# Scoring part of batch 0 through 128x32 TensorE tiles, with a check of the row sums and a second program behind it

## The chip, the cores and the metric

The kernel runs on one core of a Trainium2 chip. A core has five engines that run side by side and meet through semaphores: TensorE (PE, matrix multiplications into PSUM, with PEld as its weight loads), VectorE (DVE), ScalarE (ACT), GpSimd (POOL) and SyncE (SP). POOL and SP start DMA transfers here, ACT two of them. PSUM has eight banks of 128 x 512 float32. The metric is the device time of one execution in microseconds (us); lower is better. Weights of a matmul are rows x columns: a "128x32 tile" multiplies with 128 rows of weights and 32 output rows, and occupies a quarter of the array.

## The reference

```python
scale = 1.0 / np.sqrt(q.shape[-1])
scores = scale * np.matmul(q, k.transpose(0, 1, 3, 2))
scores = np.einsum('bhij,hg->bgij', scores, w_pre)
scores = scores - np.max(scores, axis=-1, keepdims=True)
attn = np.exp(scores)
attn = attn / (np.sum(attn, axis=-1, keepdims=True) + 1e-09)
attn = np.einsum('bhij,hg->bgij', attn, w_post)
out = np.matmul(attn, v)                      # b, head, row, 64
x = out.transpose(0, 2, 1, 3).reshape(8 * 448, 768)
h = np.maximum(x @ w_in, 0.0)
return (h * h) @ w_out
```

8 batches, 12 heads, 448 rows, head size 64; w_in is 768 x 2048, w_out 2048 x 768. Twelve heads of scores are mixed by `w_pre` ahead of the softmax and by `w_post` behind it. The subtraction of the row's maximum cancels in exact arithmetic; it keeps the exponential in range.

## The kernel before

**The scheme.** The program is planned by itself. Python code emits tasks with costs and dependencies; `_Plan` places them. TensorE's order is written out by hand: `ORDER` is a string in which each digit names one of ten streams (0 transposes, 1 QK, 2 pre, 3 post, 4 AV, 5 direct, 6 and 7 FFN-in, 8 and 9 FFN-out), and the next unit of that stream goes next. The planner gives copies out of PSUM to ACT or DVE, whichever ends earlier by its costs, and picks the PSUM banks. Every engine then runs its list in order.

**Attention.** The 448 rows of a batch are cut into 45 chunks of ten rows, so that a chunk has 10 x 12 heads = 120 rows of scores. For most chunks three steps make the scores. `emit_QK` multiplies a tile of rows by all keys, one pair of heads at a time, and copies the result into `stage`, rows on partitions (lines 460 and 461 are the copy helper, on ACT and on DVE). `emit_rel` moves a chunk by DMA from SP (line 954) to `dring`, with heads and rows of the chunk on 120 partitions. `emit_pre` (line 977) mixes the heads there with `wk1`, in 64x64 tiles. Behind it, `after_pre` takes the exponential with the row sum (ACT, line 994), the reciprocal (line 1008), and folds it into the `w_post` weights (line 1015, POOL). `emit_post` (line 1047) transposes and mixes again, with two copies into `a2t`. `emit_AV` (lines 1104 and 1125) multiplies by v. The exponential is taken without the maximum.

**The first 22 chunks of batch 0** go another way, since there is no earlier batch whose FFN could run beside them. `emit_scale` (line 834, DVE) multiplies q with `w_pre` into `w_out_sb` and `h2t`, which are not in use yet; `emit_direct` (line 856) adds up six full matmuls of 128x128 over 448 keys, which yields mixed scores in the layout of a chunk at once, without QK, relay and pre. The exponential reads that bank.

**FFN.** `emit_F1` multiplies by w_in (for batches 0 and 1 in whole 128x128 matmuls, line 1173; behind them in pairs of 64-row halves, line 1194), then relu (lines 1225 and 1226) and the square (line 1235) into `h2t`. `emit_F2` multiplies by w_out in halves (line 1316), `emit_last` the last two tiles whole (line 1265). The forms of tiles in use are called full (128x128), row (two of 64x128), quad (four of 64x64) and cols (two of 128x64).

Of the kernel before, what the change touches and what calls it, by code (L numbers as in the profile page):

```python
# [8 lines left out]
DT = mybir.dt  # L9
# [14 lines left out]
EVENTS = {"tr": 0.12, "qk": 0.72, "di": 0.2, "po": 0.61, "pr": 1.1, "av": 0.43, "o0": 0.43}  # L24
# [3 lines left out]
INF = float("inf")  # L28
ORDER = (
    "0001155500055555555555555555513155511155555331555533355551135555552005113555555330023324"  # L30
    "2443310041316261116722326772267633227713367333761142441114223667227631167713226671136713"
    "3277620029333912293921812283383338240024442002661118111833381118132672226773136713376224"
    "2444227761136711166333620027622813822383383337771422444200116667733002277622181183118133"
    "8339122922933912291191139333924244422163613731711631622007227363216372227610016733720208"
    "1383338113822291911393119224244422383138311831384222444223621617311716331620027337226336"
    "2127372001636217337220093191119131922833831181138242444222919313933392242444228318331811"
    "1833622267317216362200733733622167200173622367131720029319131931192228181338113822283833"
    "1842244442444238161336220073373362226761171716337610026733724244412812283382020839111911"
    "3913392291192229319138333811382424442283611673317622673137163167122762226733791229339213"
    "98338242444228338338222868633837226773667733677646444876766776678766776879989999899888"  # L40
# [12 lines left out]
class _Task:  # L53
# [3 lines left out]
                 "done", "bias", "sync", "group", "instrs", "issued", "later", "two")  # L57

    def __init__(self, name, engine, fn, deps, after, cost, prio, sem, seminc, mode, dma,
# [18 lines left out]
        self.sync = ()  # L78
        self.done = self.issued = False
# [9 lines left out]
class _Group:  # L89
# [4 lines left out]
    def __init__(self, n):  # L94
        self.n = n
        self.banks = None
        self.readers = [[] for _ in range(n)]


class _Plan:  # L100
# [44 lines left out]
    def _commit(self, t, e, start):  # L145
# [5 lines left out]
        self.free[e] = start + held  # L151
        t.end = start + lat
# [93 lines left out]
    def _commit_pe(self, t, start):  # L246
        if t.mode != self.mode:
            self.mode = t.mode
        g = t.group
        if g is not None and g.banks is None:  # L250
            _, got = self.find(g.n, self.free[PE])
            g.banks = sorted(got)
            for i, readers in zip(g.banks, g.readers):
                for d in self.bank_users[i]:
                    if d not in t.deps:
                        t.deps.append(d)
                self.bank_users[i] = readers
                self.age += 1
                self.bank_age[i] = self.age
# [8 lines left out]
    def next_unit(self, order, at):  # L268
        if at >= len(order):
            return None  # L270
        t = self.streams[int(order[at])][0]
        if t.nwait:
            return None
        est = max(self.free[PE], t.avail)
        if t.group is not None and t.group.banks is None:
            est = max(est, self.find(t.group.n, self.free[PE])[0])
        if t.mode != self.mode:
            est = max(est, self.free[PE] + MODE_SWITCH)
        return (est, t) if est < INF else None

    def run(self, order=""):
        self.start()
        at = 0
        while True:
# [15 lines left out]
            if f is not None and (best is None or f[0] <= best[0]):  # L300
# [3 lines left out]
                self.streams[int(order[at])].pop(0)  # L304
                at += 1
                self._commit_pe(f[1], f[0])
# [12 lines left out]
def bass_talking_heads_attention__then__ffn_squared_relu_kernel(  # L319
# [18 lines left out]
    ND = 22  # L338
    NDW = 16
    DH = 4  # L340
# [23 lines left out]
    with ExitStack() as es:  # L364
# [12 lines left out]
        NFULL = 2  # L377
# [8 lines left out]
        wq = sb("wq", [128, NP, H, H5], DT.bfloat16)  # L386
        wall = sb("wall", [128, NP, 2, H], DT.float32)
# [5 lines left out]
        rowsum = sb("rowsum", [128, NPS, 1], DT.float32)  # L393
# [17 lines left out]
        zrow = sb("zrow", [128, S], DT.bfloat16)  # L411
# [4 lines left out]

        def Sm(name):
            return _Sem(nc.alloc_semaphore(name), name)
# [5 lines left out]
        sem_z = Sm("dz")  # L424
        sem_qk = [[Sm("dqk%d_%d" % (i, x)) for x in range(2)] for i in range(3)]
        sem_v = Sm("dv")
        sem_wq = Sm("dwq")
# [3 lines left out]
        sem_last = Sm("olast")  # L431
        sem_out = [Sm("oslot%d" % i) for i in range(NOS)]

        plan = _Plan(NB)

        def c_pe(t):
            return {PE: (t, t + 190.0)}

        def c_ev(cols):
            return {ACT: (cols / 1.2 + 65.0, cols / 1.2 + 175.0),  # L440
                    DVE: (cols / 0.96 + 72.0, cols / 0.96 + 160.0)}

        def add(name, engine, fn, deps, cost, prio, mode=None, group=None, instrs=0):
            return plan.add(name, engine, fn, deps, cost, prio, "ctr", 1, mode, group=group,
                            instrs=instrs)

        events = {}

        def unit(s, name, fn, deps, ns, mode, group, mms):
            kind = name[:2]  # L450
            was = events.get(kind, 0.0)
            events[kind] = was + EVENTS.get(kind, 0.5)
            n = 2 * mms + int(events[kind]) - int(was)
            t = add(name, PE, fn, deps, c_pe(ns), 0, mode, group, n)
            s.append(t)
            return t

        def copy(eng, en, o, i_):
            if en == ACT:
# [1051 lines left out]
```

## Time and profile before

| | us |
|---|---|
| median of 3 runs | 526.3 (523.89 to 526.61) |
| the profiled execution | 521.03 |
| its span, first to last instruction | 519.0 |
| ACT exponentials, 360 | 191.1 busy, 555 ns each |
| PE FFN-out in halves, 1664 | 152.0 busy |
| PE FFN-in in halves, 1344 | 121.9 busy |
| DVE copies into a2t, 192 | 117.3 busy |

The page gives for each engine the busy time and its share of the span; then the span in 40 slices, a digit for tenths:

```profile
PE   7998999999999999999999999999999999999997
DVE  6966989889889677978897778975897668865430
ACT  3688999889988889898998889988878886887310
PEclk9999999999999999999999999999999999999999
```

The clock of TensorE was granted in full throughout. The chain of work is followed back from the last instruction: at each step to what released it, or to the instruction before it on its engine. Busy time of PE holds the latency of its last matmul, so neighbouring rows overlap.

### The profile page before, as it was taken

What the parts mean: (1) busy time and instruction counts of PE and PEld (TensorE: products, weight loads), DVE (VectorE), ACT (ScalarE), POOL (GpSimd) and SP (SyncE); (2) the same over time, 40 slices, a digit from 0 to 9 for tenths busy, and PEclk for the clock granted to TensorE, in tenths of its full rate; (3) what the DMA queues carried; (4) which work ended last, traced back from release to release, by engine and by line L of the source; (5) the groups of instructions that cost most, each with busy time, mean ns of one, the idle gap of its engine ahead of it and who ended that gap; (6) DMA issues with size and microseconds to landing.
All of it is one profiled execution on the core that took longest, in us unless ns stands there. A gap on an engine that the chain in (4) does not pass through costs nothing.

```text
span 519.0 us, 23210 instructions
## 1 busy us (share of the span) xinstructions
PE 505.7 (97%) x9632; PEld 320.0 (62%) x9632; DVE 397.4 (77%) x999; ACT 418.5 (81%) x1206; POOL 204.1 (39%) x404
## 2 busy tenths in 40 slices
PE   7998999999999999999999999999999999999997
PEld 3455767577776564666555665566556565568874
DVE  6966989889889677978897778975897668865430
ACT  3688999889988889898998889988878886887310
POOL 9913445425651455134632357124722332332000
PEclk9999999999999999999999999999999999999999
DMA  8999999746984689647984679537965557632003
GB/s 156 198 217 170 187 192 194 168 109 146 167 177 106 144 162 183 134 87 164 175 163 91 141 165 182 128 72 156 192 103 111 125 131 139 123 87 66 4 23 99
DMA packets 82560, 71.85 MB, mean 138 GB/s; under 512 B 13434, under 2 KB 79946, under 8 KB 82458
## 3 DMA queue, kind: packets, MB, share of 16 engines
q0 software_dynamic: 36944, 32.81, 38.8%
q1 hardware_dynamic: 45226, 37.38, 30.1%
q8 instruction: 77, 1.26, 1.0%
q10 hardware_dynamic: 288, 0.20, 0.1%
q14 instruction: 25, 0.20, 0.1%
HBM read 45.70 MB, written 11.01 MB: 109 GB/s over the span
## 4 chain that ended last, share of the span: by engine, by line
PE 87%; DMA 5%; DVE 4%; ACT 2%; issue 1%; SPq 1%; POOL 0%; POOLq 0%; DVEq 0%
PE ps L1316 26%; PE ps L1194 18%; PE ps L1047 7%; PE ps L977 7%; PE ps L1173 6%; PE ps L1125 6%; PE ps L908 6%; PE ps L856 5%; DMA dring<-stage 3%; PE ps L1265 2%; DVE stage L461 2%; PE ps L759 1%; DMA qraw<-in_q_dram 1%; PE ps L1104 1%; ACT pring L994 1%
## 5 line engine op out<-in xcount | busy, mean ns | idle before, releaser
L994 ACT ACTIVATE pring<-ps 128x448 bf16<-128x448 f32 x360 | 191.1, 555 | 16.3 <-PE ps L977 10.3
L1316 PE MATMUL ps<-w_out_sb,h2t 64*128 64x384 bf16 x1664 | 152.0, 323 | 0.6 <-issue 0.6
L1015 POOL TENSOR_TENSOR wk2s<-wk2b,rinv 128x120 bf16<-128x120 bf16 (+1 forms) x179 | 69.8, 392 | 189.8 <-DVE rinv L1008 188.6
L461 DVE CAST a2t<-ps 128x480 bf16<-128x480 f32 (+1 forms) x192 | 117.3, 640 | 14.7 <-PE ps L1047 13.2
L1194 PE MATMUL ps<-xt,w_in_sb 64*128 64x448 bf16 (+2 forms) x1344 | 121.9, 323 | 0.2
L461 DVE CAST stage<-ps 128x448 bf16<-128x448 f32 (+1 forms) x174 | 104.5, 617 | 15.4 <-PE ps L908 11.5
L460 ACT ACTIVATE stage<-ps 128x448 bf16<-128x448 f32 (+1 forms) x186 | 96.6, 551 | 23.0 <-PE ps L908 21.1
L1316 PEld LDWEIGHTS ps<-w_out_sb,h2t 64*128 64x128 bf16 x1664 | 77.1, 94 | 52.4 <-issue 3.6
L460 ACT ACTIVATE a2t<-ps 128x480 bf16<-128x480 f32 (+1 forms) x176 | 92.8, 574 | 13.6 <-PE ps L1047 13.2
L1194 PEld LDWEIGHTS ps<-xt,w_in_sb 64*128 64x128 bf16 x1344 | 62.2, 94 | 40.4 <-PE ps L977 2.2
L1348 POOL DMA_DIRECT2D out_dram<-osb x59 | 37.1, 634 | 111.3 <-ACT pring L994 42.2
L994 ACT ACTIVATION_READ_ACCUMULATOR pring<-ps 128x1 f32 x360 | 79.0, 219 | 0.0
L1047 PEld LDWEIGHTS ps<-wk2s,pring 60*128 60x128 bf16 x2880 | 56.1, 93 | 21.4 <-issue 3.1
L1047 PE MATMUL ps<-wk2s,pring 60*128 60x60 bf16 x2880 | 61.1, 187 | 1.0 <-issue 0.3
L1226 DVE TENSOR_SCALAR h1t<-ps 128x448 bf16<-128x448 f32 (+2 forms) x102 | 49.0, 488 | 16.5 <-PE ps L1194 14.1
L1008 DVE RECIPROCAL rinv<-rowsum 128x2 f32<-128x2 f32 (+1 forms) x184 | 29.1, 158 | 35.9 <-ACT pring L994 35.0
L977 PE MATMUL ps<-dring,wk 60*64 60x448 bf16 (+1 forms) x676 | 54.5, 362 | 1.5 <-DVE stage L461 0.6
L1235 DVE TENSOR_TENSOR h2t<-h1t 128x448 bf16<-128x448 bf16 (+2 forms) x176 | 52.6, 332 | 0.5 <-ACT h1t L1225 0.2
L908 PE MATMUL ps<-qkt 64*128 64x448 bf16 (+1 forms) x360 | 49.8, 354 | 1.4 <-issue 1.4
L1225 ACT ACTIVATE h1t<-ps 128x448 bf16<-128x448 f32 (+2 forms) x74 | 32.9, 456 | 19.7 <-PE ps L1194 18.0
L1173 PE MATMUL ps<-xt,w_in_sb 128*128 128x220 bf16 (+1 forms) x384 | 41.7, 260 | 0.1
L1173 PEld LDWEIGHTS ps<-xt,w_in_sb 128*128 128x128 bf16 x384 | 34.6, 98 | 5.7 <-DVE h1t L1226 0.9
(59 smaller groups left out, 419.3 us busy)
## 6 DMA issues: line engine op xcount, KB each, us to landing
dring<-stage SPq DMA_DIRECT2D x309, 105.0 KB
out_dram<-osb POOLq DMA_DIRECT2D x45, 192.0 KB, 4.0
qraw<-in_q_dram POOLq DMA_DIRECT2D x42, 112.0 KB, 5.5
kraw<-in_k_dram POOLq DMA_DIRECT2D x42, 112.0 KB, 5.3
w_in_sb<-in_moe_w_in_dram POOLq DMA_DIRECT2D x8, 384.0 KB, 12.7
w_out_sb<-in_moe_w_out_dram POOLq DMA_DIRECT2D x8, 384.0 KB, 8.7
vraw<-in_v_dram POOLq DMA_DIRECT2D x21, 128.0 KB, 5.1
vraw<-in_v_dram POOLq DMA_DIRECT2D x21, 96.0 KB, 5.3
```

Source lines behind the costliest of these rows:

```text
L460: return eng.activation(o, i_, AF.Copy)
L461: return eng.tensor_copy(o, i_)
L908: r_ = eng.matmul(ps[y * w:(y + 1) * w, g.banks[x], 0:S], qkt[r0:r0 + 64, pb, p + y, 0, i0:i0 + w], qkt[r0:r0 + 64, pb, p + y, 1, :], star ...
L977: r_ = eng.matmul(ps[64 * y:64 * y + 64, gr.banks[x], 0:S], wk1[64 * x:64 * x + 64 - R0 * x, :], dring[64 * x:64 * x + 64 - R0 * x, (g0 + ...
L994: return eng.activation(pring[:, pr, 0:S], ps[:, gr.banks[x], 0:S], AF.Exp, accum_out=rowsum[:, pr, :])
L1015: return eng.tensor_tensor(wk2s[:, p0:p0 + n, :], i0.to_broadcast([128, n, PR]), rinv[:, p0:p0 + n, :].to_broadcast([128, n, PR]), ALU.mult)
L1047: r_ = eng.matmul(ps[:, gr.banks[x], o0:o0 + PR], pring[64 * x:64 * x + PR, pr + y, j0:j0 + 2 * PJ], wk2s[64 * x:64 * x + PR, pr + y, :], ...
L1173: r_ = eng.matmul(ps[:, g.banks[0], 0:n], w_in_sb[:, ft, t * 128:(t + 1) * 128], xt[:, ft, c0:c1], start=(ft == 0), stop=(ft == NFT - 1))
L1194: r_ = eng.matmul(ps[:, g.banks[x], 0:n], w_in_sb[64 * y:64 * y + 64, ft, t * 128:(t + 1) * 128], xt[64 * y:64 * y + 64, ft, c0:c1], start ...
L1226: return eng.tensor_scalar(h1t[:, s, 0:n], ps[:, g.banks[x], 0:n], 0.0, None, op0=ALU.max)
L1235: return eng.tensor_tensor(h2t[:, t16, o0:o0 + n], h1t[:, s, 0:n], h1t[:, s, 0:n], ALU.mult)
L1316: r_ = eng.matmul(ps[:, g.banks[hh], 0:FH], h2t[64 * y:64 * y + 64, t16, col:col + 128], w_out_sb[64 * y:64 * y + 64, t16, hh * FH:(hh + 1 ...
```

## The change

Five things change together.

1. Thirty chunks of batch 0 (`ND` 22 to 30) go a new way. `emit_spread` copies q into `qz`, a zeroed part of `h2t`, so that for each chunk and pair of heads ten columns stand in one of eight places of 32 columns, zero elsewhere. `emit_spr` multiplies in eight matmuls of 128x32 weights, two for each of four column groups, accumulated; one copy brings the bank to `dring`; `emit_pre` mixes it with `wkf` in one full matmul. The products with `w_pre` and `emit_direct` are gone, and so are the zeroing of `dring` by DMA and the load of `w_pre` to all partitions; four small loads bring `wrepf`.
2. The remaining 15 chunks of batch 0 are scored as before, from two tiles of rows.
3. Every QK unit of 128 rows, every FFN-in pair and every FFN-out tile but the last two can be run in two forms; the letters a to j in `ORDER` choose the other one (quad for QK, full for the FFN). The order is new throughout.
4. Row sums of all chunks are kept. At the end DVE tests that each lies between 1e-30 and 1e30, a DMA from SP turns the 128 results into one row, and a last reduction makes a flag.
5. The whole program is built twice; the second one takes the row's maximum first. Each engine runs up to a point near its end, waits for the flag, loads it, and either jumps behind the second program and ends its list, or ends its list and runs the second program. PE does that behind its last unit; ACT from tasks planned 4 us behind the flag, DVE 8 us, POOL 0.5, SP 0.

```diff
-    ND = 22
+    ND = 30
+EVENTS = {..., "sp": 0.3, ...}
+TURN = {ACT: 4000.0, DVE: 8000.0, POOL: 500.0, SP: 0.0}
...
+            def emit_spread(p):
+                for x, (k, o) in enumerate(places(p)):
+                    def fn(eng, en, x=x, k=k, o=o):
+                        rows = slice(64 * x, 64 * x + 64)
+                        i_ = qkt[rows, 0, p, 0, 0:ND * CH].rearrange("p (c a) -> p c a", a=CH)
+                        return copy(eng, en, qz[rows, :, k, o:o + CH], i_)
...
+            def emit_spr(c, parts):
...
+                    for n, col, p in todo:
+                        r_ = eng.matmul(ps[32 * col:32 * col + 32, g.banks[0], 0:S],
+                                        qz[:, c, 2 * col + n, :], qkt[:, 0, p, 1, :],
+                                        start=(n == 0), stop=(n == 1))
...
+                def fn_sev(eng, en):
+                    return copy(eng, en, dring[:, c % NDS, :], ps[:, g.banks[0], 0:S])
...
-                    r_ = eng.matmul(ps[:, g.banks[0], 0:S],
-                                    qs[:, p, y:y + 2, :].rearrange("p i g -> p (i g)"),
-                                    qkt[:, 0, p, 1, :],
-                                    start=(p == 0), stop=(p == NP - 1 if len(ps_) == 3
-                                                          else p == 5))
...
 def fn_pre(eng, en):
+    if g0 < ND:
+        for g in gs:
+            r_ = eng.matmul(ps[:, gr.banks[g - g0], 0:S],
+                            wkf[:, :, :].rearrange("p i g -> p (i g)"),
+                            dring[:, g % NDS, :], start=True, stop=True)
+        return r_
...
+                def fn_max(eng, en):
+                    return eng.tensor_reduce(nmax[:, pr, :], ps[:, gr.banks[x], 0:S], AX.X, ALU.max,
+                                             negate=True)
...
+                t_in = add("good0", DVE, fn_in, list(exp_of.values()) + used,
+                           {DVE: (450.0, 550.0)}, 1e8)
+                t_in = add("good1", DVE, fn_both, [t_in], {DVE: (450.0, 550.0)}, 1e8)
+                t_in = add("good2", DVE, fn_least, [t_in], {DVE: (450.0, 550.0)}, 1e8)
+                t_turn = plan.add("turn", SP, fn_turn, [t_in], {SP: (780.0, 2800.0)}, 1e8, sem_good, 16)
+                t_flag = add("flag", DVE, fn_flag, [t_turn], {DVE: (200.0, 300.0)}, 1e8)
...
+        fast, fast_waits, t_flag = program(False)
+        slow, slow_waits, _ = program(True)
...
+            emit_tasks(eng_name, eng, tasks[:k], fast_waits)
+            eng.wait_ge(t_flag.sem.handle, t_flag.semval)
+            fine = eng.value_load(flag[0:1, 0:1])
+            with eng.If(fine == 0):
+                emit_tasks(eng_name, eng, tasks[k:], fast_waits)
+                for s_, v_ in reached:
+                    eng.wait_ge(s_.handle, v_)
+                emit_tasks(eng_name, eng, slow[eng_name], slow_waits)
+            if k < len(tasks):
+                with eng.Else():
+                    emit_tasks(eng_name, eng, tasks[k:], fast_waits)
```

Counted in the built programs, up to the flag: TensorE 9632 matmuls before and 9486 after (132 full ones of the direct scoring go, 240 of 128x32 and 30 full ones come); SP's relays from `stage` to `dring` 367 and 359; 30 copies of 128x448 and 12 of 64x300 come, 36 products on DVE go.

1826 lines of the change are left out of this document (962 added, 864 removed).

## The prediction

> **What bounds the kernel now.** I read the page first (busy shares, then the chain that ended last), then the busy time by stretches, then the first 50 us and the tail in order of time.
>
> ```profile
> span 519.0 us, 23210 instructions
> PE 505.7 (97%) x9632; PEld 320.0 (62%) x9632; DVE 397.4 (77%) x999; ACT 418.5 (81%) x1206; POOL 204.1 (39%) x404
> PE 87%; DMA 5%; DVE 4%; ACT 2%; issue 1%; SPq 1%; POOL 0%; POOLq 0%; DVEq 0%
> ```
>
> TensorE (PE) is the bound: it holds 87% of the chain and idles 13.3 us in all. A busy PE is not yet a PE at its pace, so the price of a unit is taken below from the start of one unit to the start of the next. A second limit shows only when the early part is cut out:
>
> ```profile
> 13.00:52.00 39.00, 36.94 (x623) 20.40 (x617) 29.87 (x84) 30.92 (x89) 17.89 (x32) 1.00 1.14 195
> 52.00:65.00 13.00, 13.00 (x220) 9.35 (x215) 12.54 (x41) 12.64 (x42) 6.32 (x12) 1.00 1.02 187
> 65.00:78.00 13.00, 12.06 (x208) 8.79 (x206) 11.04 (x33) 11.87 (x36) 5.49 (x12) 1.00 1.03 192
> 78.00:91.00 13.00, 12.89 (x274) 10.07 (x272) 12.30 (x38) 12.38 (x40) 7.43 (x16) 1.00 1.04 194
> 13.00:91.00 78.00, 74.90 (x1313) 48.61 (x1307) 65.75 (x193) 67.81 (x205) 37.12 (x70) 1.00 1.09 193
> ...
> 481.00:494.00 13.00, 13.00 (x246) 11.24 (x244) 5.41 (x20) 3.81 (x9) 0.00 (x0) 1.00 0.02 4
> ```
>
> The columns are PE, PEld, DVE, ACT, POOL, clock, DMA share. From 13 to 91 us DVE and ACT together hold 133.6 of 156 us (86%), and 97%, 88% and 95% in the three last stretches: that is the neighbourhood into which the change puts new evacuations. At 481 us, in the last FFN, they are nearly idle.
>
> **The change, part by part.** First the scoring of batch 0.
>
> ```profile
> 13.30 7.48 PE ps L856 x39
> 105.71 2.00 PE ps L1125 x40
> 458.85 0.38 PE L977 MATMUL ps<-dring,wk 64*64 64x448 bf16 x4
> 459.06 0.36 PE L1104 MATMUL ps<-a2t,vraw 64*64 64x220 bf16 x8
> 459.25 0.36 PE L977 MATMUL ps<-dring,wk 64*64 64x448 bf16 x4
> 459.55 1.13 PE L1125 MATMUL ps<-a2t,vraw 128*64 128x220 bf16 x20
> 57.74 1.80 PE ps L1173 x18
> 485.79 5.99 PE L1194 MATMUL ps<-xt,w_in_sb 64*128 64x220 bf16 x120
> ```
>
> A full 128x128 matmul over 448 columns costs 7.48/39 = 0.192 us. Removed: 22 chunks x 6 = 132 of them, 25.3 us. Added: eight 128x32 matmuls a chunk. No such tile is in the trace. If four run side by side, a chunk takes two rounds of 0.192, and the first six chunks, cut into three units each, take three: 24 x 2 + 6 x 3 = 66 rounds, 12.7 us. If they ran one by one it would be 240 x 0.192 = 46.1 us. The nearest row is L1125: 40 matmuls in 128x64 tiles take 2.00 us, 0.050 each, where 220 columns alone at the pace of 0.192/448 would be 0.094: two do run side by side. I take 12.7. The mixing matmul that now follows (128x128 weights, one for a chunk) adds 30 x 0.192 = 5.8. Net -6.8 us.
>
> [...]
>
> Chunks 22 to 29 no longer go through the relay and its 64x64 mixing: four units fewer at 0.21 (start at 458.85 to start at 459.06), -0.8. Sixteen score units take the 64x64 form at that 0.21 in place of 0.19 (two half-row matmuls side by side at 0.192): +0.2, between 0 and 0.4.
>
> The new order: between units of one tile form nothing is lost (459.06 to 459.25), but 64x64 to 128x64 takes 0.30, 0.1 more. Counted in the two programs' TensorE orders, changes of form go from 245 to 276: in the part ahead of the first FFN matmul from 34 to 70, behind it 209 to 204. +31 x 0.1 = +3.1 us. FFN units switched between whole and half-row form cost the same (1.80/18 = 0.100; 2 x 5.99/120 = 0.100). PE's sum: -6.8 - 0.8 + 0.2 + 3.1 = -4.3 us, between -5 and -3.5.
>
> Now ACT and DVE.
>
> ```profile
> L461 DVE CAST stage<-ps 128x448 bf16<-128x448 f32 x127 | 75.7, 615 | 11.1 <-PE ps L908 10.0 <-PE ps L1047 0.3
> L460 ACT ACTIVATE stage<-ps 128x448 bf16<-128x448 f32 x149 | 76.9, 555 | 19.4 <-PE ps L908 18.0 <-issue 1.1
> L1235 DVE TENSOR_TENSOR h2t<-h1t 128x228 bf16<-128x228 bf16 x48 | 12.1, 284 | 0.1
> 0.00:13.00 13.00, 3.51 (x9) 1.00 0.87 156
> 13.00:91.00 78.00, 10.05 (x28) 1.00 1.09 193
> 1.97 0.24 DVE L519 MEMSET zrow<- 4x224 uint32 x1
> 8.20 0.63 PE L755 MATMUL ps<-ident,kraw 64*64 64x64 bf16 x28 [1.94 <-DMA kraw<-in_k_dram]
> ```
>
> (The two rows with x9 and x28 are L834, the products of q with the weights, by stretch.) Thirty new evacuations of 128x448 at the mean of 615 and 555 ns: +17.6 us. Twelve spread copies of 64x300, taken as 0.3 each from the 284 ns row, half of them behind 13 us: +1.8. The small weights: +0.5. The products go: -10.1. Net +9.8 us on two engines behind 13 us. Ahead of it the zeroing of qz, 1920 words by 0.24/224, is 2.1 us on DVE and about as much on ACT; the cover is PE's wait for k, which ends at 8.20 whatever DVE does, and without it the first transposes would start up to 1 us later. I take 0.
>
> So from 13 us on the two engines have 143.4 us to do where PE's path is 78 - 4.3 = 73.7 us long: 97.3% busy. They have held 97% for 13 us and 95% for 13 us, and 88% between. At 96%, the mean of the two better stretches, the part takes 143.4/1.92 = 74.7: **1.0 us of the 4.3 is given back**. That is my value; the bounds are 0 (work of batch 1 is put off to where they have room) and 7.8 (at 88%, 81.5 us).
>
> Small loads: four more come ahead of wrep and wrep2 on SP.
>
> ```profile
> 5.43 0.97 SPq L528 DMA_DIRECT2D wrep<-in_w_pre_dram  x1
> 6.45 1.62 SPq L531 DMA_DIRECT2D wrep<-in_w_post_dram  x2
> 15.85 0.21 DVE L565 TENSOR_TENSOR wk2b<-wrep,mask 60x60 bf16<-60x60 f32 x1
> wall<-in_w_pre_dram SPq DMA_DIRECT2D x1, 72.0 KB, 5.8
> out_dram<-osb SPq DMA_DIRECT2D x6, 96.0 KB, 2.2
> vraw<-in_v_dram POOLq DMA_DIRECT2D x6, 48.0 KB, 8.6
> ```
>
> At 0.8 each they push the last issue from 8.1 to 11.3 us; with 5.8 to land, that is 17.1 against a use at 15.85. DVE would stop up to 1.3 us, with dring evacuations queued behind it, while ACT goes on. I take 0 and keep 1.3 for the range. The loads of w_out, which no longer wait for the scoring, still wait for the mixing of the same chunks: 0.
>
> The check of the row sums. Three DVE passes over 128x368 (about 0.5 each by the 615 ns row) and a 1x128 one sit between the last squares, where DVE is busy 5.41 of 13 us; the turn of the 128 values is one DMA on an SP that has no relay left. Without that cover they would cost 2 us. Then each engine loads the flag and jumps over the second program.
>
> ```profile
> 48.72 0.35 PE L908 MATMUL ps<-qkt 64*128 64x448 bf16 x1
> 50.51 0.36 PE L908 MATMUL ps<-qkt 64*128 64x448 bf16 x1 [1.44 <-issue]
> ...
> 488.31 0.36 ACT L1225 ACTIVATE h1t<-ps 128x228 bf16<-128x228 f32 x1 [1.40 <-PE ps L1194]
> 504.91 10.57 PE L1265 MATMUL ps<-w_out_sb,h2t 128*128 128x384 bf16 x64
> 515.52 0.49 ACT L460 ACTIVATE osb<-ps 128x384 f32<-128x384 f32 x1 [5.23 <-PE ps L1265]
> ```
>
> A jump is not in the trace. PE once stood 1.44 us inside a unit with nothing that it waited for; a DMA lands in 2.2 us when the queues are quiet and 8.6 when full. So 1.4 to 8.6 us, and I take 2.2, since at 481 us DMA is at 0.02. ACT jumps after the third relu of the last half. By the new order PE then has two FFN-out units of 8 matmuls (10.57/64 = 0.165, 1.3 each) and seven FFN-in units in the seven free banks (0.6 each): some 6.9 us that need nothing of ACT, an estimate. DVE jumps after the eighth square, with about as much. PE jumps behind its last matmul, where the last evacuation (515.52) and its transfer run to 519.0: 3.5 us. So 0.
>
> [...]
>
> **Sum:** -4.3 + 1.0 = -3.3 us, span 515.7. The profiled execution took 521.03 (2 us around its span), below the three shown (523.89 to 526.61); put on their median it is 523.0.
>
> **Rivals.** (1) ACT and DVE take everything back, at 92 to 93%: 143.4/1.85 = 77.5 against 78, so 525.8. The 88% stretch speaks for it, the 97% stretch against. (2) The other side: they become the bound in batch 0 outright. At 88%, what 65 to 78 us shows, the part takes 81.5 us, +3.5: 529.8. It decides from 91.9% (143.4/156) downwards. For it: three engines now pass each chunk along, score, evacuation, mixing, exponential, so banks are held longer; against: eight relays of 105 KB fewer where the DMA share is above 1. (3) The jumps are on the path. At 8.6 us each, ACT and DVE exceed their cover by 1.7 each and PE the end by 5.1: +8.5, time 531.5; slower than before from a jump of 6.8 us. Against: DMA is idle there. (4) More than forecast: the engines never bind, and the 2.1 us that PE idles from 13 to 52 (36.94 of 39) go with the relays: -4.3 - 2.1 = -6.4, 519.9. (5) The change doesn't do what it says: the 32-column tiles run one by one (+33.4, 556), or a flag sends all into the second program (about twice the time).
>
> **How the numbers follow.** Chances: forecast 0.40, rival 1 0.16, rival 2 0.20, rival 3 0.07, rival 4 0.14, rival 5 0.03. A measurement of this kernel tells about 0.5%, 2.6 us, from no change; the forecast's own range is 521.3 to 524.0, a tenth of it inside that band. Faster: 0.36 + 0.14 = 0.50; same: 0.16 + 0.04 = 0.20; slower: 0.20 + 0.07 + 0.03 = 0.30. The range runs from below rival 4 to between rivals 2 and 3: 518.5 to 531.
>
> **What would show it.** The 32-column rows: a full chunk's eight start 0.38 to 0.40 us apart from the next; 1.5 shows rival 5. Mixing starts 0.19 apart. The first FFN matmul, at 53 us before, comes 4 to 6 us earlier. DVE plus ACT from 13 to 87 us stand near 96%; PE idle for evacuations of dring, with the two near 90%, is rival 2. A gap on ACT or DVE near 485 us that PE answers with a gap of its own, or a time from the last matmul to the end well over 3.5 us, is rival 3. It is wrong if PE's span up to its last matmul does not shrink by 2 to 5 us.

## The result, and the profile after

| | before | after |
|---|---|---|
| median, 10 executions each, us | 524.6 (521.8 to 529.5) | 532.0 (529.8 to 538.4) |
| ratio after / before | | 1.0119 [1.0086, 1.0153] |

A median counts all executions; a ratio compares only those within 1.5% of their kernel's fastest. The change makes the kernel slower by 1.2%, some 6 to 8 us; the forecast was 523.0, and 532.0 lies just above its range of 518.5 to 531.

The two profiles are further apart than the medians. The one of the kernel before is from an execution of 521.0, shorter than all ten above, and the one of the changed kernel is from its longest (538.4). A second profile of the changed kernel, further down, is from one of 538.8 and has the same kinds of losses. So their sizes below are larger than in a middling execution.

The page of the changed kernel first: span, busy time of the engines, one queue (packets, MB, share), and the chain that ended last.

```profile
span 536.3 us, 22918 instructions
PE 509.0 (95%) x9486; PEld 316.9 (59%) x9486; DVE 397.5 (74%) x985; ACT 431.3 (80%) x1232; POOL 204.0 (38%) x404
...
q8 instruction: 78, 1.28, 1.0%
...
PE 76%; ACT 9%; DMA 8%; DVE 3%; issue 2%; SPq 0%; ACTq 0%; DVEq 0%
```

PE's part of the chain fell from 87 to 76%; ACT's rose from 2 to 9 and DMA's from 5 to 8. PE is held up more often, and by more kinds of work.

Next, the order of time on PE: three scored chunks, the first FFN matmul, and three attention-by-v units that both kernels have.

```profile
24.55 1.32 PE L910 MATMUL ps<-qkt,h2t 128*32 128x448 bf16 x24
25.80 0.66 PE L1138 MATMUL ps<-wk2s,pring 60*128 60x60 bf16 x32
...
28.88 0.93 PE L1047 MATMUL ps<-dring,wkf 128*128 128x448 bf16 x4
29.74 0.56 PE L910 MATMUL ps<-qkt,h2t 128*32 128x448 bf16 x8
...
47.59 0.74 PE L1266 MATMUL ps<-xt,w_in_sb 128*128 128x220 bf16 x6
...
102.04 0.38 PE L1195 MATMUL ps<-a2t,vraw 64*64 64x220 bf16 x8
130.85 0.37 PE L1195 MATMUL ps<-a2t,vraw 64*64 64x228 bf16 x8
497.48 0.39 PE L1195 MATMUL ps<-a2t,vraw 64*64 64x228 bf16 x8
```

The same in the kernel before (its first FFN matmul starts at 52.96):

```profile
52.96 0.74 PE L1173 MATMUL ps<-xt,w_in_sb 128*128 128x220 bf16 x6
...
104.48 0.36 PE L1104 MATMUL ps<-a2t,vraw 64*64 64x220 bf16 x8
126.35 0.37 PE L1104 MATMUL ps<-a2t,vraw 64*64 64x228 bf16 x8
481.40 0.39 PE L1104 MATMUL ps<-a2t,vraw 64*64 64x228 bf16 x8
```

Three chunks take 1.25 us (25.80 - 24.55), 0.42 each, and the mixing 0.215 a chunk (0.86/4). The FFN starts 5.4 us earlier. At the third attention unit the changed kernel is still 2.4 us ahead, at the fourth 4.5 behind, at the last 16.1. What happens between the third and the fourth is in two views, the order of time on PE and the busy time by stretches (length, then PE, PEld, DVE, ACT, POOL, granted clock, DMA share, GB/s):

```profile
105.27 0.31 PE L831 MATMUL ps<-ident,kraw 64*64 64x64 bf16 x14
108.95 0.31 PE L831 MATMUL ps<-ident,kraw 64*64 64x64 bf16 x14 [3.37 <-issue]
```

```profile
106.00:108.00 2.00, 0.00 (x0) 0.00 (x0) 0.00 (x0) 0.43 (x2) 0.10 (x1) 1.00 0.58 149
108.00:110.00 2.00, 1.05 (x23) 0.81 (x24) 0.69 (x2) 0.51 (x1) 0.00 (x0) 0.91 0.33 74
110.00:112.00 2.00, 2.00 (x13) 1.22 (x13) 1.05 (x3) 0.74 (x3) 0.39 (x1) 0.50 0.06 8
```

In the middle of 28 transposes PE stands for 3.37 us and waits for nothing that the profile shows; then the granted clock is 0.50 for 3.4 us, so the work done in them takes 1.7 us longer. This stop has a place: counting PE's matmuls, weight loads and semaphore instructions in order, the stops put down to "issue" with over 0.35 us of idle time, in every profile of this study, fall 193 to 195 behind a multiple of 256. So I take them for the ends of blocks of 256 instructions. The planner of both kernels counts such blocks too (`BLOCK = 256` and `fetch_wait`, with a count that begins at 63, so that the first one ends 193 instructions later). The row of the instruction queue fits: 78 transfers, 1.28 MB, 16.4 KB each, about one for each 256 of PE's 19,580. Of the 76 such places in this profile, five show an "issue" stop of over 0.65 us from one start to the next; this one is the longest.

The other kind of stop, at 266 us: the chain of waits, ACT, DVE and PE in order of time, and the stretches.

```profile
261.44 7.80 DMA dring<-stage
```

```profile
269.39 2.10 ACT L519 ACTIVATE stage<-ps 64x448 bf16<-64x448 f32 x4 [3.57 <-DMA dring<-stage]
...
269.42 0.62 DVE L520 CAST stage<-ps 64x448 bf16<-64x448 f32 x1 [4.25 <-DMA dring<-stage]
...
270.42 0.58 PE L1138 MATMUL ps<-wk2s,pring 60*128 60x60 bf16 x16 [3.54 <-ACT stage L519]
```

```profile
268.00:270.00 2.00, 0.00 (x0) 0.00 (x0) 0.58 (x2) 0.61 (x2) 0.00 (x0) 1.00 0.67 150
270.00:276.00 6.00, 5.36 (x68) 2.73 (x69) 5.25 (x12) 4.43 (x11) 2.28 (x4) 0.51 0.78 141
```

ACT and DVE are both to copy scores into `stage`. It has two slots, so the copies wait for the relays of the tile two back, which have not landed. Behind the waiting copy nothing else on either engine can run, and PE's next unit waits for a bank that such a copy frees; when it goes on, the clock is halved for over 6 us. The waits of all such copies together (total, times, longest), after:

```profile
ACT stage L519 <- DMA dring<-stage: 9.2, 5, 3.6
DVE stage L520 <- DMA dring<-stage: 6.8, 5, 4.2
```

and before:

```profile
DVE stage L461 <- DMA dring<-stage: 0.7, 1, 0.7
```

**An account of PE's time**, worked out from the matmul rows of each trace. Where two neighbouring matmuls start more than 0.65 us apart, the distance is a stop: of the kind "block" when the profile puts it down to issue, "relay" when a copy into `stage` or a relay ended it, else "other". "Clock" is the time below the full granted clock times what was missing. What is left of the time to the last matmul's start is PE's work at its pace, with all waits that are too short to count.

| us | last matmul | block | relay | other | clock | PE's work |
|---|---|---|---|---|---|---|
| before | 515.2 | 3.9 | 1.7 | 2.3 | 0.0 | 507.3 |
| after | 532.3 | 9.7 | 10.4 | 4.9 | 5.1 | 502.1 |
| after, second profile | 531.4 | 12.7 | 5.7 | 6.1 | 3.4 | 503.5 |

PE's work shrank by 4 to 5 us. Stops and half clock grew from 8 us to 30 and 28, in executions 17 us apart.

### The profile page after: what moved, and what is told of

Same layout as the page of the kernel before. It is cut to its first block, busy times and chain, and to the rows that moved or that the text cites. A ratio compares the mean times of both kernels' runs of the same rounds, so it can differ in the third digit from the quotient of the medians.

```text
span 536.3 us, 22918 instructions
## 1 busy us (share of the span) xinstructions
PE 509.0 (95%) x9486; PEld 316.9 (59%) x9486; DVE 397.5 (74%) x985; ACT 431.3 (80%) x1232; POOL 204.0 (38%) x404
## 3 DMA queue, kind: packets, MB, share of 16 engines
q8 instruction: 78, 1.28, 1.0%
## 4 chain that ended last, share of the span: by engine, by line
PE 76%; ACT 9%; DMA 8%; DVE 3%; issue 2%; SPq 0%; ACTq 0%; DVEq 0%
PE ps L1407 22%; PE ps L1273 12%; PE ps L1266 10%; DMA dring<-stage 8%; PE ps L1138 6%; PE ps L1053 6%; PE ps L1216 5%; ACT pring L1077 5%; PE ps L979 5%; PE ps L1400 3%; PE ps L1349 2%; PE ps L831 2%; ACT stage L519 1%; ACT dring L519 1%; DVE stage L520 1%
## 5 line engine op out<-in xcount | busy, mean ns | idle before, releaser
L1077 ACT ACTIVATE pring<-ps 128x448 bf16<-128x448 f32 x360 | 191.9, 563 | 10.4 <-PE ps L1053 9.1
L1407 PE MATMUL ps<-w_out_sb,h2t 64*128 64x384 bf16 x1472 | 134.9, 323 | 0.0
L520 DVE CAST a2t<-ps 128x480 bf16<-128x480 f32 (+1 forms) x197 | 120.9, 642 | 13.4 <-PE ps L1138 12.2
L520 DVE CAST stage<-ps 128x448 bf16<-128x448 f32 (+1 forms) x185 | 111.7, 617 | 21.4 <-PE ps L979 11.4
L1407 PEld LDWEIGHTS ps<-w_out_sb,h2t 64*128 64x128 bf16 x1472 | 67.6, 94 | 45.5 <-issue 2.5
L1273 PE MATMUL ps<-xt,w_in_sb 64*128 64x448 bf16 (+2 forms) x936 | 86.9, 321 | 2.3 <-ACT pring L1077 1.7
L1266 PE MATMUL ps<-xt,w_in_sb 128*128 128x220 bf16 (+2 forms) x588 | 82.3, 291 | 1.9 <-issue 1.5
L1266 PEld LDWEIGHTS ps<-xt,w_in_sb 128*128 128x128 bf16 x588 | 53.9, 99 | 25.1 <-issue 4.9
L1317 DVE TENSOR_TENSOR h2t<-h1t 128x448 bf16<-128x448 bf16 (+2 forms) x176 | 53.1, 326 | 15.9 <-ACT h1t L1307 12.2
L1273 PEld LDWEIGHTS ps<-xt,w_in_sb 64*128 64x128 bf16 x936 | 42.8, 94 | 28.8 <-DVE qkt L520 1.9
L1053 PE MATMUL ps<-dring,wk 64*64 64x448 bf16 (+1 forms) x660 | 53.6, 362 | 4.0 <-DVE qkt L520 1.6
L1307 ACT ACTIVATE h1t<-ps 128x448 bf16<-128x448 f32 (+2 forms) x91 | 39.1, 443 | 18.6 <-PE ps L1266 8.3
L1308 DVE TENSOR_SCALAR h1t<-ps 128x448 bf16<-128x448 f32 (+2 forms) x85 | 42.7, 507 | 9.6 <-PE ps L1266 5.7
```

Source lines behind the costliest of these rows:

```text
L520: return eng.tensor_copy(o, i_)
L1053: r_ = eng.matmul(ps[64 * y:64 * y + 64, gr.banks[x], 0:S], wk1[64 * x:64 * x + 64 - R0 * x, :], dring[64 * x:64 * x + 64 - R0 * x, (g0 + ...
L1077: return eng.activation(pring[:, pr, 0:S], ps[:, gr.banks[x], 0:S], AF.Exp, accum_out=rowsum[:, g, :])
L1266: r_ = eng.matmul(ps[:, g.banks[ph], 0:n], w_in_sb[:, ft, t * 128:(t + 1) * 128], xt[:, ft, c0:c1], start=(ft == 0), stop=(ft == NFT - 1))
L1273: r_ = eng.matmul(ps[:, g.banks[x], 0:n], w_in_sb[64 * y:64 * y + 64, ft, t * 128:(t + 1) * 128], xt[64 * y:64 * y + 64, ft, c0:c1], start ...
L1308: return eng.tensor_scalar(h1t[:, s, 0:n], ps[:, g.banks[x], 0:n], 0.0, None, op0=ALU.max)
```

## The experiments

Each was timed together with the kernel before, on the same chip; times are medians, ratios are to the kernel before.

**1. The changed kernel again.** 

> The changed kernel once more, for a profile in which TensorE's clock is granted more evenly. Theory O (the new order of batches 1 to 7 loses the time: TensorE runs out of instructions in dense stretches and waits for relays, and its clock is halved behind the longest stops): the first FFN matmul again near 49.5 us, about 3.5 us earlier than before, and the lead gone by batch 2; stops of TensorE that wait for nothing the profile shows near 100, 105, 153 and 218 us, 6 to 8 us in all against 3.0 before. Theory G (the check and the jumps): the lead holds to 480 us and is lost behind it. Time 530 to 533 us.

Measured: 534.7, ratio 1.0189 [1.0134, 1.0243], above the expected 530 to 533. The loss is real. The lead is gone by the third attention unit (105.96 us, against 104.48 in the kernel before), as theory O has it and theory G has not. The block stops come to 12.7 us by the account, more than expected, and the longest, 3.62 us at 65 us, stands at another place than in the first profile.

**2. Without the check and the jumps.**

```diff
-            emit_tasks(eng_name, eng, tasks[:k], fast_waits)
-            eng.wait_ge(t_flag.sem.handle, t_flag.semval)
...
+            emit_tasks(eng_name, eng, fast[eng_name], fast_waits)
```

> Leaves out the test of the row sums, the second program and the jumps; scoring and order as in the changed kernel. Theory O: within 1.5 us of the changed kernel. Theory G: back by 5 us or more, to about 525.

Measured: 534.8, 1.0190 [1.0136, 1.0245], level with run 1; both intervals are some 3 us wide to either side. Within that, the check, the flag and the second program cost nothing. The tail of the changed kernel shows the cover:

```profile
505.31 1.92 PE L1266 MATMUL ps<-xt,w_in_sb 128*128 128x228 bf16 x18
507.31 0.36 ACT L1307 ACTIVATE h1t<-ps 128x228 bf16<-128x228 f32 x1 [2.62 <-PE ps L1266]
513.18 1.92 PE L1266 MATMUL ps<-xt,w_in_sb 128*128 128x228 bf16 x18
513.89 0.28 DVE L1317 TENSOR_TENSOR h2t<-h1t 128x228 bf16<-128x228 bf16 x1 [3.16 <-issue]
```

ACT is away for 2.62 us and DVE for 3.16; PE has FFN units to run through both. DVE's gap is the jump. ACT's ends with a wait for PE, and without the jump it is 1.99 us at the same place, so its jump took at most 2.6.

**3. The old order behind the new start.** The order of the changed kernel up to its first FFN unit, from there the order of before. 

> The changed kernel with its order up to the first FFN unit, and behind it the order and the forms of units of the kernel before; scoring, check and second program stay. Theory O: 3 us faster than the kernel before, 520 to 523. Rival S (the new scoring costs the time, by the evacuations of dring or the relays that follow): no faster than the changed kernel, 530 or more.

Measured: 542.0 beside 524.4 for the kernel before, from four executions: 532.7, 541.9, 542.1 and 547.2. No ratio was formed from them. Theory O's 520 to 523 is missed by all four; rival S's "530 or more" is met. Since one execution is level with the changed kernel, it is not shown that this order is slower still. The waits of the copies, in the execution of 541.9:

```profile
DVE stage L520 <- DMA dring<-stage: 10.4, 4, 6.6
ACT stage L519 <- DMA dring<-stage: 8.1, 4, 5.7
```

So late relays are not a matter of the new order alone.

**4. Blocks shifted.** Six warm-up matmuls at the start become 70 short ones, 64 more matmuls in all.

```diff
-                    for _ in range(n):
+                    for _ in range(n - 6 if now < 2500.0 else n):
...
+                    for _ in range(70 if now < 2500.0 else 0):
+                        r_ = eng.matmul(ps[0:128, g.banks[0], 0:8], warm[:, 0:128], warm[:, 0:8],
+                                        start=True, stop=True)
```

> The changed kernel with 64 more matmuls in the first warm-up (six of 448 columns less, seventy of 8 more), so that all later TensorE instructions stand 128 places later in the stream; nothing else changes. If the stops of 1.25 and 3.37 us inside the transposes near 100 and 105 us are the ends of loaded blocks of instructions, they move to other units: at most one stop remains between 98 and 110 us, below 2 us, and others show elsewhere; time within 4 us of the changed kernel, either way. Rival: they wait for something of their own (a bank, a copy); then they stay at the same units with the same lengths.

> The kernel before with the same 64 more matmuls in its first warm-up, so that its blocks of 256 TensorE instructions end 128 places later; order, scoring and forms untouched. Theory F (where a block ends decides: the kernel before runs with only 3.0 us of stops because its order fits its own block ends): 2 to 8 us slower than before, with stops of over 1.5 us at places 193 to 195 of a block and clock drops behind them. Rival: the kernel before stands well with any block ends, within 1.5 us of 524.4, and the changed kernel's stops have another reason.

Measured: the changed kernel 534.2, 1.0175 [1.0098, 1.0252]; the one before 526.7, 0.9973 [0.9919, 1.0027]. In the changed kernel the stops at 102 and 109 us are gone, and others stand elsewhere: 2.35 us in the transposes at 51 us, 1.46 at 150, again 193 and 194 behind a multiple of 256. This ties the stops to the blocks' ends, and it leaves the time of the changed kernel within the noise: a shift moves the ends, it does not spare them. (The planner does not see the 64 matmuls; it still counts the ends at the old places.)

In the kernel before, the shift brought what theory F expects of the stops. Its profile, of an execution of 531.5, has three of over 2 us:

```profile
PE ps L1128 <- issue: 2.4, 1, 2.4
PE ps L762 <- issue: 2.4, 2, 2.1
PE ps L1197 <- issue: 2.1, 1, 2.1
```

By the account these and a shorter one come to 9.2 us, and the clock is halved behind two of them. So block stops as large as the changed kernel's need neither the new scoring nor the new order. Whether the shift costs the kernel before any time is not settled: its ten executions run from 519.5 to 531.5, and by medians it is some 2 us slower (526.7 beside 524.9).

**5. Without loads.** q, k and v of batches 2 to 7 are not loaded; the rest runs on old data.

```diff
-                        if b != 1:
-                            emit_load_qk(b)
+                        if b >= 2:
+                            for a in range(3):
+                                qk_tasks[(b, a)] = []
+                        elif b != 1:
+                            emit_load_qk(b)
```

> The kernel before without the loads of q, k and v for batches 2 to 7 (they compute on the rows of batch 1); the comparison for the next one. Theory D (stops for instructions and for late relays come from transfers that share the DMA engines with the loads): no stop of TensorE over 0.8 us behind 100 us, 518 to 523 us. Without that: unchanged near 524.

> The changed kernel without the same loads. Theory D: stops over 1.5 us and waits for the relays into dring gone behind 100 us, no clock drop there; the lead of about 3.5 us at the first AV is kept, so 2 to 4 us faster than the kernel before without loads. Rival: still 5 us or more slower than it, so the loss lies in the work itself (changes of tile form, copies).

Measured: before 518.4, 0.9877 [0.9847, 0.9908]; after 520.9, 0.9922 [0.9893, 0.9951]. The two are 2.5 us apart and not 7 to 10. So most of the loss needs the loads beside it: the copies' waits for relays fell from 16.0 us to the one row

```profile
ACT stage L519 <- DMA dring<-stage: 0.9, 1, 0.9
```

What stays is 9.0 us of block stops against 2.4, all between 44 and 110 us (0.84, 1.69, 1.40, 1.70 and 2.25 idle).

**6. The new scoring for 22 chunks, in the order of before**, with the mixing units put in. 

> The new scoring for 22 chunks alone, as many as before, with the order and forms of the kernel before (a mixing matmul inserted one pair of chunks behind each score), check and second program kept. TensorE's work falls by 22 x (1.15 - 0.58) = 12.5 us less some 4 us for changes of form, DVE and ACT get 12.9 us of copies for 13.7 us of products. If the scoring is sound and the loss comes from blocks and relays, the first AV comes 5 us or more earlier and the time is 517 to 527, by how the block ends fall; if the scoring itself is what costs, 530 or more.

Measured: 543.1, 1.0305 [1.0202, 1.0408]; not 517 to 527, and the first attention unit comes later than before (47.84 against 46.51 us), not 5 us earlier. The copies wait 20.3 us for relays (12.2 on DVE and 8.1 on ACT).

A second order with the new scoring, and the same kinds of loss: PE's work is 504.5 by the account, less than before, and stops and half clock come to some 30 us.

**7. The new order with the old scoring.** The kernel before, with the changed kernel's order behind its own first FFN unit (the units have the forms of before, since it has no others). 

> The kernel before, its own scoring of 22 chunks and its own order up to the first FFN unit, then the order of units of the changed kernel. Theory O (the new order of the units behind the scoring is what costs: it lets the scores' copies run into relays that have not landed, at the units of 267, 336 and 387 us of the changed kernel): first FFN matmul where it is before (53 us), the waits on the relays come back at the same units, and the time is 530 to 536. Theory S (the loss comes from the new scoring itself, whose instructions are denser: blocks run out in the first 110 us and everything behind is out of step): no stop over 1.5 us ahead of 110 us, no late relays, time 523 to 527.

Measured: 541.5, 1.0338 [1.0298, 1.0378].

```profile
ACT stage L460 <- DMA dring<-stage: 1.6, 2, 0.8
DVE stage L461 <- DMA dring<-stage: 0.4, 1, 0.4
```

Slower than theory O's 530 to 536, and not for its reason: the copies wait 2.0 us for relays, not 16. By the account PE's work is 517.9, 10 more than before. There are 40 more changes of tile form than before, some 4 us at 0.1 each, and PE's idle time in waits too short for the account is 6.3 us against 2.5; the rest is open. So these four cases stand, in us of waits of copies on relays: old scoring with old order 0.7, old with new 2.0, new with new 16.0, new with old 18.5. In these profiles late relays come with the new scoring, whatever the order. This run says nothing clean about the new order in the changed kernel, since that one has the second forms.

**8. A third slot.** `stage` gets three slots. To make room for it, only half of w_out is loaded, and used twice; the first run has that alone.

```diff
-        stage = sb("stage", [IT, 2, H, S], DT.bfloat16)
+        stage = sb("stage", [IT, 3, H, S], DT.bfloat16)
...
-                sl = n % 2
-                old = rel_of.get(n - 2, [])
+                sl = n % 3
+                old = rel_of.get(n - 3, [])
```

> The changed kernel with only the first half of the second FFN weight loaded, and read twice (the output is not the reference's); it frees 12 KB a partition and takes 3.1 MB off the transfers between some 35 and 70 us. It is the control for the next run. Theory B (blocks of PE instructions come late because they share the queues with transfers): the stops ahead of 70 us get shorter, 1 to 3 us less in all, time 529 to 533. Theory D (the stream is simply too dense there): stops and time stay, 532 to 536.

> The run before it with a third slot in the buffer from which scores are relayed, so that a score copy waits for the relays of three tiles back and not two. Theory R (late relays hold the copies, these hold TensorE, and the clock halves behind the longer waits): the waits of the copies on the relays vanish, at the units of 267, 336 and 387 us, and 5 to 9 us come off the run before it, 523 to 528. Theory B: what is lost is lost at block ends, the relays' waits only take up slack that the blocks' stops have made; 0 to 2 us come off, 530 to 534.

Measured: control 532.2, 1.0109 [1.0058, 1.0161], which fits either theory; third slot 523.8, 0.9979 [0.9938, 1.0019]. That is 8.4 us by the medians, 6.8 by the ratios, and the kernel is level with the one before. The copies' waits in the control:

```profile
DVE stage L520 <- DMA dring<-stage: 7.4, 6, 3.4
ACT stage L519 <- DMA dring<-stage: 6.6, 4, 2.7
```

With the third slot the view has no such row left, and the longest rows of PE are:

```profile
PE ps L831 <- issue: 4.0, 3, 2.3
PE ps L1053 <- DMA dring<-stage: 1.9, 1, 1.9
```

Block ends come first now. This is the experiment that shows the larger cause: theory R expected 5 to 9 us, theory B 0 to 2.

**9. Without loads and half of w_out.** 

> The changed kernel without the loads of q, k and v of batches 2 to 7 and without the second half of the second FFN weight (the output is not the reference's). The one without the q, k, v loads alone had 7.9 us of stops at block ends, all between 44 and 110 us. Theory B (those blocks are late because transfers share the queues): with less to transfer between 35 and 70 us the stops there fall under 3 us and the time to 515 to 518. Theory D (the stream of the new scoring is too dense for the loading of blocks, whatever else runs): 6 to 8 us of stops, 520 to 522.

Measured: 518.2, 0.9868 [0.9816, 0.9920]: between the two expectations, with 4.9 us of block stops instead of 9.0. That may be the fewer transfers, though profiles of one kernel swing as much; and the stop of 2.81 us in the transposes at 104 us is as long as ever, while the queues are not full (the DMA share, the last number but one):

```profile
100.00:104.00 4.00, 3.50 (x117) 2.90 (x120) 2.33 (x6) 3.09 (x10) 2.58 (x5) 1.00 0.67 106
104.00:107.00 3.00, 0.24 (x28) 0.13 (x15) 0.29 (x2) 1.09 (x4) 0.39 (x2) 0.87 0.62 170
```

How much is density and how much sharing stays open.

**10. A third slot for the old order.** Here half of w_in is left out, since the kernel before uses w_out's buffer.

> The kernel before with only the first half of the first FFN weight loaded, and read twice (the output is not the reference's), to free 12 KB a partition: the control for the runs beside it. Both theories: the first FFN units do not wait for the weight today, so 520 to 526.

> The run before it with a third slot in the relay buffer. Theory R (the new order alone makes copies meet relays that have not landed; the order of before has its relays in time): nothing to gain, within 2 us of the control. Theory G (a third slot helps any order, and the changed kernel's loss has another cause that it merely makes up for): 4 to 8 us less than the control.

> The scoring of before, the changed kernel's order of units behind it, half of the first weight, and a third slot. Without the third slot this pairing of scoring and order took 541.5 us. Theory R: the third slot takes off as much as it did with the new scoring, 6 to 9 us, 532 to 536, and the new order stays slower than the old one by what the new scoring would have gained and by its changes of tile form. Theory M (an order fits only the scoring that it was made for, whatever the relays do): under 3 us come off, 538 to 542.

> The new scoring up to the first FFN unit, the order of before behind it, half of the first weight, a third slot. Without the slot this took 542.0, with a wait of 6.5 us for a relay at 325 us and three halved clocks behind stops. Theory R (relays are what the earlier start collides with): the waits on relays go, and the lead of 3.3 us at the first FFN unit is kept but for block stops, 520 to 527. Theory M: it stays above 533.

Measured: control 524.3, 0.9994 [0.9960, 1.0028]; with the slot 526.1, 1.0009 [0.9973, 1.0044]. The kernel before has nothing to gain from it, as theory R says. (The profile with the slot has 9.6 us of block stops and the one without 3.8, the same scoring and order in both.) Old scoring with new order and slot: 537.2, 1.0264 [1.0182, 1.0346], 4 us less than without, between R and M. New scoring with old order and slot: 532.3 (525.0 to 534.9), 1.0068 [1.0021, 1.0116], 10 less by the medians, yet not below before, between R and M again. No copy waits for a relay any more; PE itself still waits 2.9 us for relays, and 7.9 us of block stops and two halved clocks are left. So with the slot each order is level with the kernel before under the scoring that it was written for, and not under the other.

**11. Later relays in the plan.** The complete kernel; the planner counts a relay as landed later and so puts other work ahead of the copies.

```diff
-DMA_END = {"move": 2800.0, "load": 2300.0}
+DMA_END = {"move": 4300.0, "load": 2300.0}
```

> The changed kernel, complete, with one number of its planner raised: it counts a relay as landed 4.3 us behind its transfer and not 2.8, so that it puts other work ahead of copies into the relay buffer on ScalarE and VectorE; TensorE's order is the same. Theory R: the copies wait shorter in front of the engines' other work, the stops at 266 and 336 us shrink, 525 to 530. Theory Q: the copies only go elsewhere in the queues, TensorE waits for the scores that come later by it, 531 to 536.

> The same with 5.8 us. Theory R: the waits of 3 us for a relay are gone, 522 to 528, level with the third slot. Theory Q: no better than the run beside it, 531 to 538.

Measured: 529.8, 1.0143 [1.0071, 1.0216], inside theory R's range, and 537.4, 1.0292 [1.0207, 1.0378], inside theory Q's. In the first the copies wait 7.6 us for relays, against 16.0 and 9.5 in the two profiles of the changed kernel, but its interval does not tell it from that kernel; the second has 8.3 and a new wait of 3.4 us for another copy. These two plans do not take the loss back. No complete version found here beats the kernel before.

The account for the runs that carry the argument:

| us | last matmul | block | relay | other | clock | PE's work |
|---|---|---|---|---|---|---|
| before, no loads | 510.9 | 2.4 | 0.8 | 0.8 | 0.0 | 506.9 |
| before, half w_in | 515.1 | 3.8 | 0.0 | 2.7 | 0.0 | 508.6 |
| before, half w_in, third slot | 520.6 | 9.6 | 0.0 | 1.0 | 0.0 | 510.0 |
| before, blocks shifted | 525.6 | 9.2 | 2.3 | 1.9 | 3.4 | 508.9 |
| after, no loads | 516.6 | 9.0 | 1.0 | 0.0 | 1.7 | 504.9 |
| after, half w_out | 523.5 | 5.4 | 9.9 | 2.5 | 1.7 | 504.0 |
| after, half w_out, third slot | 518.7 | 5.9 | 2.1 | 2.3 | 3.4 | 505.0 |
| new scoring, old order | 534.9 | 9.5 | 8.7 | 5.2 | 8.5 | 503.0 |
| old scoring, new order | 535.3 | 5.3 | 2.7 | 7.6 | 1.7 | 517.9 |

In the row of the new scoring with the old order, 1.9 us of the half clock lie inside a stop and are counted twice.

## Why the prediction was wrong, point by point

**Right: the pace of the 128x32 tiles.** Four run side by side (four start within 10 ns, the next four 0.2 us later): three chunks and the change of form behind them take 1.25 us, 0.42 a chunk, against 0.38 to 0.40 forecast without that change, and one by one it would have been 1.5. The weight loads, 95 ns each in the mean, do not run one after another: the first eight start within 25 ns, and all 24 in a row would alone take 2.3 us.

**Right, as far as the account can tell: PE's sum.** -4.3 was forecast. The account has 506.9 to 510.0 for five profiles of the old kernel and its cut versions, 508.3 in the mean, and 500.9 to 507.0 for eight of the changed one (with runs 2, 4 and 9), 504.0 in the mean: -4.3, from profiles that spread over 3 and 6 us. The FFN starts 5.4 us earlier, inside the forecast of 4 to 6, but only in part for its reason: ahead of its first FFN matmul the old kernel has 4.1 us of stops in this profile (a wait for k of 2.3 us, a block end of 1.8), and the changed one has none.

**Near, with the term too small: ACT and DVE in batch 0.** By stretches of the changed kernel:

```profile
13.00:52.00 39.00, 38.02 (x782) 18.23 (x784) 36.37 (x92) 37.12 (x112) 20.10 (x37) 1.00 1.15 190
52.00:65.00 13.00, 12.86 (x267) 9.68 (x262) 12.65 (x39) 12.93 (x40) 4.96 (x10) 1.00 1.11 200
65.00:78.00 13.00, 11.84 (x214) 9.36 (x213) 9.36 (x31) 11.15 (x36) 9.08 (x17) 1.00 1.03 188
78.00:91.00 13.00, 12.71 (x264) 8.93 (x260) 11.49 (x34) 12.00 (x40) 4.68 (x10) 1.00 0.91 186
13.00:91.00 78.00, 75.42 (x1512) 46.20 (x1514) 69.86 (x192) 73.20 (x224) 38.83 (x73) 1.00 1.09 191
```

69.86 + 73.20 is 143.1 where 143.4 was forecast; part of that is luck, since the changed kernel is some 2 to 5 us further on within the same stretch. Of the single terms, the 30 new copies took 16.5 us (17.6 forecast). The two engines are 94% busy from 13 to 52 us and 98% from 52 to 65. By 102 us the lead of 5.4 us at the first FFN matmul had shrunk to 2.4: 3 given back, where I took 1.0 and bounded it by 7.8; the block stop of 1.25 us just ahead of that unit is part of the 3. Rival 2, these engines as the bound, is not what made the kernel slow: it was ahead at 102 us in this profile, and in the second one, 1.5 behind by then, a block stop of 3.6 us and the half clock behind it stand in between. That its 529.8, like rival 3's 531.5, lies near the result is luck: neither mechanism came.

**Right: the check and the jumps at 0** (run 2). DVE's jump took 3.2 us and ACT's at most 2.6, forecast 2.2, inside the cover; that a jump takes as long as a DMA's landing in quiet queues was an estimate; from the last matmul's start to the end it is 4.0 us, 3.8 before.

**Wrong: the sum itself.** "-4.3 + 1.0 = -3.3 us, span 515.7" takes over from the kernel before its 13.3 us of PE idle time and its full clock, as if they were properties of the chip. They belonged to that one arrangement of units, relays, loads and blocks. The term for what a new arrangement does to them was missing, and it is the largest: stops and half clock went from 7.9 to 30.2 us in the profiled execution, +22, against -5 of work. In the medians, 7.4 us slower with some 4 less work, it is about +11, an estimate. The order was priced by its changes of form alone (+3.1). The relays from `stage` got no term at all; they stand only in rival 2, as eight fewer. And the block ends got none, although the planner has a figure for them.

**What stood in its place**, by size. First, copies into `stage` that meet relays not yet landed: a third slot takes off 6.8 us, shown, in a pair of kernels with half of w_out. Second, stops at block ends. Without loads they are 9.0 us against 2.4, and that is most of the stops that then stay; but the old kernel has between 2.4 and 9.6 us of them in its five profiles and the changed one between 4.9 and 12.7, so it is not shown that the change makes them longer on the whole. Third, the clock halved behind some stops (1.7 to 5.1 us in the account of the changed kernel and its cut versions).

The row of 1.44 us with nothing waited for was in the prediction, read only as a bound for a jump. It is such a stop itself, 193 behind a multiple of 256. From 13 to 52 us the change puts 782 matmuls where 623 were; that this density makes the blocks late is argued and not shown, since most of the stops come behind that part and the shifted kernel of before has them without it.

**Open:** why the new scoring makes the relays late from 260 us on, long after the part that it changes. The queues are as full there in the kernel before (DMA share 0.96 from 262 to 266 us, against 0.92). That it does so under two orders, only with loads beside it, and not with a third slot, is shown; by which shift of loads against relays is not.

## What to carry to other kernels

Idle time and clock of a tuned kernel are not constants to subtract from (here stops and half clock went from 8 to 30 us): if an edit moves the order of units, ask of every buffer with two slots how much time its transfers had to spare, and give the sum a term for using that up. Where a planner counts a cost, as this one counts blocks, look at what it holds before you price a change. To see whether late transfers or the work itself costs the time, compare both kernels without the loads, and then with one more slot. If a stop waits for nothing, count its place in the engine's instructions: here such stops stood 193 to 195 behind a multiple of 256, also with 64 more matmuls ahead, and the time with these was 534.2 us, beside 532.0 and 534.7 without. The shift identified them and did not cure them.

## What was unexpected of the hardware

The granted clock falls to 0.50 for 3.4 us, or 6.8, behind some stops (of 3.37 and 3.54 us in the changed kernel), so such a stop costs half as much again or more. Stops of 2.3 us were followed by it in one run (third slot, 104 us; mean granted clock 0.993) and not in another (old kernel with the slot, 374 us; 1.000), so the length alone does not decide it. A stop of 1.44 us is the shortest case: at the same QK unit, it was followed by the half clock with the new order and the old scoring (first line) and not in the kernel before (second; the granted clock is the last number but two).

```profile
54.00:56.00 2.00, 2.00 (x29) 0.74 (x26) 1.59 (x3) 1.71 (x4) 0.00 (x0) 0.50 1.26 255
54.00:56.00 2.00, 2.00 (x24) 1.43 (x21) 2.00 (x8) 2.00 (x8) 0.16 (x1) 1.00 0.76 150
```
